# Per-head logits by way of DRAM instead of selector matmuls, in a fused sliding-window attention and gated-MLP kernel

## The chip, the cores and the metric

The kernel runs on one core of a Trainium2 chip. The metric is device time in microseconds (us), the median of several executions. A core has TensorE (PE in the profile, the matmul array), VectorE (DVE), ScalarE (ACT), GpSimd (POOL) and SyncE (SP, which here issues nearly all DMA; ACT has two entries in the profile's list of issues). The profile lists each engine's instructions apart, and for a wait it names the instruction or the DMA that ended it. The program is written as a list of steps. A scheduler in the build lays the steps of each engine into one static order.

The kernel before took 1630.06 to 1631.79 us in its four runs beside the changed kernel.

## The reference, cut to what matters

```python
def _A_ref(x, wqkv, wo):                  # attention: H = 32 heads of 32 columns
    W, dil = 8, 2                         # each token looks at 8 positions, 2 apart
    ...                                   # q, k, v from x @ wqkv; kg, vg: k, v at the 8 positions
    logits = einsum("bhsd,bhswd->bhsw", q, kg) * scale
    attn = softmax(where(mask, logits, -1e9), axis=-1)
    return einsum("bhsw,bhswd->bhsd", attn, vg) ... @ wo

def _B_ref(x, W_gate, W_up, W_down):      # D = 1024, F = 3584
    gate = x @ W_gate;  up = x @ W_up
    return (relu(gate) * up) @ W_down

x = x + _A_ref(_layernorm(x), wqkv, wo)   # S = 2048 tokens
x = x + _B_ref(_layernorm(x), ...)
x = x + _A_ref(...);  x = x + _B_ref(...) # the same two again
```

## The kernel before

The 2048 tokens are cut into four blocks of 512, and the pair of layers runs twice, so there are eight blocks, 0 to 7. TensorE works through them without a pause: q/k and v projections, output projection (wo), gate/up, down. The attention of block n+1 is computed on DVE while TensorE does the gate/up stage of block n. A gate/up stage has 28 steps. Each step is two groups of eight 128x512 matmuls (acc_g, acc_u), a ReLU on ACT and one product on DVE, called hT. The product is what frees the PSUM buffer of acc_u.

Below are the parts that the change and the argument touch; cuts are marked with "...".

```python
psum = tile_pool(name="psum", bufs=6, space=PSUM)     # acc_g, acc_u, acc_q, acc_k, ... share six buffers

def red_mm(n, prod, first, last):         # selector matmuls: sum the 32 columns of each head
    ...                                   # L: logits, partition = (token quarter, head)
    for wh in range(2):
        for tq in range(TPB):
            mm(st["L"][32*tq:32*tq+32, WH*wh:WH*(wh+1), :], lhsT=sel[:],   # sel is 128x32
               rhs=prod[:, WH*wh:WH*(wh+1), tq*P:(tq+1)*P], ..., tile_position=(0, 32*tq))

def softmax(n):
    Lt = st["L"]                                                            # in PSUM
    ...
    nc.vector.tensor_reduce(m[:], Lt[:].rearrange("p w t -> p t w"), axis=AX.X, op=ALU.max)
    nc.vector.tensor_tensor(d[:], Lt[:], _ap(m, 0, [[0, W], [1, P]]), op=ALU.subtract)
    nc.scalar.activation(d[:], d[:], ACT.Exp, scale=scale)
    ...                                                                     # ssum, reciprocal rs, a
def pv_steps(n): ...       # 8 steps: attention times v, and its sum over the window, all on DVE

def gu_steps(n, ln):
    def f_(j):
            ...
            for nm in ("g", "u"):
                acc = psum.tile([P, BLK], F32, tag="acc", name=f"acc_{nm}")
                ...                                                         # eight matmuls
                if nm == "g":
                    r = pool["hid"].tile([P, BLK], BF16, tag="r", name="r", bufs=3)
                    tail_act[0] = nc.scalar.activation(r[:], acc[:], ACT.Relu).ins
            nc.vector.tensor_tensor(hold["hT"][:, j, :], accs["u"][:], r[:], op=ALU.mult)

def sp_dma(dst, src, transpose=False):    # all on SyncE, in the order of the program's text:
    with tc.issue_after(tail_sp[0]):      # issue_after fixes the order of two instructions
        tail_sp[0] = start(dst, src).ins  # of one engine, and nothing else

# where the steps are emitted (n: the block whose gate/up starts at "at"; us)
        spread(gu, at, 2 * GRP)           # GRP = 1.73, one group of eight matmuls
        ...
        elif n + 1 < NN:
            ev.append((at + 0.1, reds_n[n + 1]))
            ev.append((at + 0.2, lambda n=n: softmax(n + 1)))
            spread(pv_steps(n + 1), at + 12.0, 6.5)
            ev.append((at + 72.0, store_o(n + 1)))
            ev.append((at + 72.1, load_o(n + 1)))
```

## Time and profile before

| | before |
|---|---|
| time, median | 1630.3 us |
| span of the profiled run | 1628.4 us |
| TensorE busy | 1618.6 us |
| all waits of TensorE on other engines | 3.3 us |
| DVE busy | 1062.6 us |

The first lines of the profile page of the kernel before (part 1, busy time; part 2, two of the strips of 40 slices, in tenths; part 4, the chain that ended last):

```profile
PE 1618.6 (99%) x7589; PEld 782.2 (48%) x7638; DVE 1062.6 (65%) x926; ACT 506.1 (31%) x1050; POOL 255.7 (16%) x220
...
DVE  5799899985497927949179492894818958211211
...
PEclk9999999999999999999999999999999999999999
...
PE 95%; DVE 4%; issue 1%; DMA 0%; POOL 0%; DVEq 0%
```

TensorE is the bound. DVE is free a third of the time on average, but the strip shows that it works in bursts, at 90% or more in some slices. Here is the full list of TensorE's waits (line, tile, what released it; total us, times, longest):

```profile
PE scratch L129 <- DVE ones L296: 1.5, 1, 1.5
PE dacc L129 <- DVE x L700: 0.8, 1, 0.8
PE acc_v L129 <- DVE xnT_first L103: 0.6, 1, 0.6
PE tp L364 <- DVE xn_first L103: 0.4, 1, 0.4
```

Three of the four lie in the first 10 us. Nothing on DVE delays the gate/up stages. The reason is in DVE's timeline at the start of such a stage (start, duration, operation, in brackets the idle time before it and what ended it). The softmax comes right after the first product, and every product stands close behind the matmuls that feed it (the fourth, at 346.36, is the latest of those shown, by 2.8 us):

```profile
332.57 0.69 DVE L673 TENSOR_TENSOR hT<-acc_u,r 128x512 bf16<-128x512 f32 x1 [2.83 <-PE acc_u L129]
333.18 1.21 DVE L565 TENSOR_REDUCE m<-L 128x128 f32<-128x1024 f32 x1
...
336.68 0.69 DVE L673 TENSOR_TENSOR hT<-acc_u,r 128x512 bf16<-128x512 f32 x1 [1.02 <-PE acc_u L129]
337.28 1.90 DVE L570 TENSOR_REDUCE ssum<-d 128x128 f32<-128x1024 f32 x1
...
341.35 0.68 DVE L673 TENSOR_TENSOR hT<-acc_u,r 128x512 bf16<-128x512 f32 x1
341.95 4.48 DVE L603 TENSOR_TENSOR pv<-a,vhm 128x4096 bf16<-128x4096 bf16 x2
346.36 0.68 DVE L673 TENSOR_TENSOR hT<-acc_u,r 128x512 bf16<-128x512 f32 x1
```

What a selector group costs is read from TensorE's timeline. The distance from acc_u to the next acc_g is 1323.85 - 1321.48 = 2.37 us with a selector group between them, where a group of eight alone takes 1.73, so the selector group costs about 0.65:

```profile
1321.48 1.89 PE L129 MATMUL acc_u<-xnT_b,w_u 128*128 128x512 bf16 x8
1323.30 0.62 PE L129 MATMUL L<-s,sel 128*32 128x512 bf16 x8
1323.85 1.90 PE L129 MATMUL acc_g<-xnT_b,w_g 128*128 128x512 bf16 x8
```

### The profile page before, as it was taken

Reading aid. Unit: us, or ns where it says so; the run is one execution under the profiler, and the core shown is the slowest. Engines: PE = TensorE matmul, PEld = TensorE weight load, DVE = VectorE, ACT = ScalarE, POOL = GpSimd, SP = SyncE. Lnnn points to the kernel's source line nnn. Section 1 sums busy time; section 2 is a strip of 40 time slices with the busy share of each in tenths; the row PEclk is TensorE's granted clock in tenths of the full one; section 3 lists DMA queues with packets and bytes.
Section 4 is the critical chain, followed back from the end, with each engine's and each line's share of the span. In section 5 each row is a group of like instructions: output and inputs, shape, how many; then the busy total and the mean of one; then the engine's idle time right before and its main releaser. Section 6 shows DMA issues by size and latency. Waiting matters only on the chain.

```text
span 1628.4 us, 18703 instructions
## 1 busy us (share of the span) xinstructions
PE 1618.6 (99%) x7589; PEld 782.2 (48%) x7638; DVE 1062.6 (65%) x926; ACT 506.1 (31%) x1050; POOL 255.7 (16%) x220
## 2 busy tenths in 40 slices
PE   9999999999999999999999999999999999999999
PEld 6644445444544445444454444544445444444444
DVE  5799899985497927949179492894818958211211
ACT  4754313243241513405134051331513311131110
POOL 2421003310250102201052010520105100000000
PEclk9999999999999999999999999999999999999999
DMA  9579656746476485664857647577484764655451
GB/s 303 93 203 252 167 177 199 192 156 200 136 215 175 155 233 171 184 175 150 229 181 185 187 150 225 162 203 212 151 231 154 194 205 155 206 164 172 156 168 65
DMA packets 371463, 296.83 MB, mean 182 GB/s; under 512 B 142512, under 2 KB 351664, under 8 KB 370480
## 3 DMA queue, kind: packets, MB, share of 16 engines
q1 hardware_dynamic: 371088, 295.23, 63.2%
q8 instruction: 60, 0.98, 0.3%
q10 hardware_dynamic: 288, 0.39, 0.1%
q14 instruction: 27, 0.22, 0.0%
HBM read 256.77 MB, written 21.00 MB: 171 GB/s over the span
## 4 chain that ended last, share of the span: by engine, by line
PE 95%; DVE 4%; issue 1%; DMA 0%; POOL 0%; DVEq 0%
PE acc_g L129 24%; PE acc_u L129 24%; PE dacc L129 22%; PE acc_v L129 7%; PE acc_k L129 6%; PE acc_q L129 6%; PE acc_wo L129 6%; DVE t L541 2%; DVE ac L551 1%; PE L L129 1%; DVE pv L603 0%; DVE x L648 0%; DVE pv L604 0%; DVE ac L541 0%; DMA x<-in_A_x_dram 0%
## 5 line engine op out<-in xcount | busy, mean ns | idle before, releaser
L129 PE MATMUL acc_g<-xnT_b,w_g 128*128 128x512 bf16 x1792 | 423.4, 379 | 0.0
L129 PE MATMUL acc_u<-xnT_b,w_u 128*128 128x512 bf16 x1792 | 423.3, 379 | 0.0
L129 PE MATMUL dacc<-w_d,hT 128*128 128x512 bf16 x1759 | 386.5, 379 | 2.5 <-DVE x L700 0.8
L672 ACT ACTIVATE r<-acc_g 128x512 bf16<-128x512 f32 x224 | 133.4, 596 | 747.1 <-PE acc_g L129 746.0
L673 DVE TENSOR_TENSOR hT<-acc_u,r 128x512 bf16<-128x512 f32 x224 | 153.7, 687 | 315.1 <-PE acc_u L129 313.5
L129 PEld LDWEIGHTS <-hT 128*128 128x128 bf16 x1792 | 175.4, 98 | 212.3 <-issue 1.0
L129 PEld LDWEIGHTS <-w_g 128*128 128x128 bf16 x1792 | 174.8, 98 | 212.7 <-issue 3.0
L129 PEld LDWEIGHTS <-w_u 128*128 128x128 bf16 x1792 | 175.4, 98 | 211.4
L541 DVE TENSOR_TENSOR t<-q,k 128x2048 f32<-128x2048 bf16 x84 | 191.7, 2290 | 8.6 <-ACT k L480 5.8
L551 DVE TENSOR_TENSOR ac<-ac,t 128x2048 f32<-128x2048 f32 x84 | 191.7, 2282 | 0.4
L485 POOL COPY kh<-k 128x14 bf16<-128x14 bf16 x64 | 81.2, 1273 | 471.9 <-ACT k L480 471.8
L700 DVE TENSOR_TENSOR x<-dacc,x 128x512 bf16<-128x512 f32 x64 | 42.5, 687 | 164.0 <-PE dacc L129 164.0
L603 DVE TENSOR_TENSOR pv<-a,vhm 128x4096 bf16<-128x4096 bf16 x64 | 145.2, 2282 | 0.0
L129 PE MATMUL acc_wo<-w_o,oT 128*128 128x512 bf16 x496 | 111.0, 379 | 0.8
L245 POOL TENSOR_TENSOR st_b<-st_b,neg_half 128x1 f32<-128x1 f32 x29 | 56.4, 1956 | 288.6 <-ACT st_b L244 288.6
L245 POOL TENSOR_TENSOR st_a<-st_a,neg_half 128x1 f32<-128x1 f32 x32 | 41.9, 1315 | 319.2 <-ACT st_a L244 319.1
L484 POOL COPY k<-kh 128x14 bf16<-128x14 bf16 x48 | 70.5, 1469 | 65.9 <-DVE t L541 43.8
L129 PEld LDWEIGHTS <-oT 128*128 128x128 bf16 x512 | 50.0, 98 | 60.4
L604 DVE TENSOR_TENSOR pv<-pv 128x2048 bf16<-128x2048 bf16 x64 | 77.4, 1215 | 0.2
L476 ACT CAST q<-acc_q 128x512 bf16<-128x512 f32 x64 | 37.3, 583 | 73.2 <-PE acc_q L129 73.2
L240 ACT ACTIVATE xn_b<-x 128x1024 bf16<-128x1024 bf16 x29 | 30.3, 1045 | 89.3 <-DVE x L648 89.3
L480 ACT CAST k<-acc_k 128x512 bf16<-128x512 f32 x64 | 37.3, 583 | 63.0 <-PE acc_k L129 62.8
(131 smaller groups left out, 1209.1 us busy)
## 6 DMA issues: line engine op xcount, KB each, us to landing
w_g<-in_B_W_gate_dram SPq DMA_DIRECT2D x56, 1024.0 KB, 7.0
w_u<-in_B_W_up_dram SPq DMA_DIRECT2D x56, 1024.0 KB, 5.4
w_d<-in_B_W_down_dram SPq DMA_DIRECT2D x48, 1024.0 KB, 5.8
w_o<-in_A_wo_dram SPq DMA_DIRECT2D x16, 1024.0 KB, 7.2
vhm<-v_d SPq DMA_DIRECT2D x32, 284.0 KB, 6.9
v_d<-vT SPq DMA_DIRECT2D x8, 1024.0 KB, 10.0
oT<-o_d SPq DMA_DIRECT2D x32, 256.0 KB, 4.4
w_d<-in_B_W_down_dram SPq DMA_DIRECT2D x16, 512.0 KB, 4.0
```

The source lines that it names most:

```text
L129: tail_pe[0] = nc.tensor.matmul(*args, **kwargs).ins
L245: nc.gpsimd.tensor_tensor(rstd, vpe, neg_half[:, 0:1], op=ALU.pow)
L476: tail_act[0] = nc.scalar.copy(q[:], acc[:]).ins
L484: nc.gpsimd.tensor_copy(k[:, 0:HALO], khalo[n - 1][:, c, :])
L485: nc.gpsimd.tensor_copy(khalo[n][:, c, :], k[:, BLK:BLK + HALO])
L541: nc.vector.tensor_tensor(t[:], i0, i1, op=ALU.mult)
L551: nc.vector.tensor_tensor(o, ac[:], t[:], op=ALU.add)
L603: nc.vector.tensor_tensor(tt[:], a_bc, v_sh, op=ALU.mult)
L604: nc.vector.tensor_tensor(tt[:, 0:4], tt[:, 0:4], tt[:, 4:8], op=ALU.add)
L672: tail_act[0] = nc.scalar.activation(r[:], acc[:], ACT.Relu).ins
L673: nc.vector.tensor_tensor(hold["hT"][:, j, :], accs["u"][:], r[:], op=ALU.mult)
L700: nc.vector.tensor_tensor(xs, ac[t], xs, op=ALU.add)
```

## The change

The intent is to take small costs off TensorE, the bound. Blocks 1 to 7 no longer use selector matmuls. Their products s go to DRAM (1 MB) and come back head-major (four loads of 256 KB in runs of 256 bytes), and DVE, which has already added the 32 columns of a head down to four partial sums, adds these four with two additions (the "head sum", u). Block 0 keeps the selector matmuls, but in two groups of four chunks. The first transposes write two PSUM tiles instead of one. The down stage's second half takes two accumulators from the logits' PSUM banks, which are free then. The last accumulator is split in two, and the last stage stores its pieces by itself. Block 1's o goes to DRAM in three stores instead of one. Below is the diff, cut:

```diff
-    ev.append((t_gu0 + 58.1, red1))
-    ev.append((t_gu0 + 58.2, lambda: softmax(1)))
+    ev.append((t_gu0 + 51.0, store_s(1)))
+    ev.append((t_gu0 + 56.0, load_s(1)))
+    ev.append((t_gu0 + 61.0, lambda: softmax(1)))
...
         elif n + 1 < NN:
-            ev.append((at + 0.1, reds_n[n + 1]))
-            ev.append((at + 0.2, lambda n=n: softmax(n + 1)))
-            spread(pv_steps(n + 1), at + 12.0, 6.5)
-            ev.append((at + 72.0, store_o(n + 1)))
-            ev.append((at + 72.1, load_o(n + 1)))
+            ev.append((at - 2.0, store_s(n + 1)))
+            ev.append((at + 3.0, load_s(n + 1)))
+            ev.append((at + 9.0, lambda n=n: softmax(n + 1)))
+            spread(pv_steps(n + 1), at + 21.0, 6.5)
+            ev.append((at + 80.0, store_o(n + 1)))
+            ev.append((at + 80.1, load_o(n + 1)))
...
+    def store_s(n):
+        def f():
+            sp_dma(s_d[n % 2][:], att[n]["s"][:].rearrange("p w t -> p (w t)"))
+    def load_s(n):
+        def f():
+            ...
+            for tq in range(TPB):
+                src = bass.AP(tensor=sd.tensor, offset=sd.offset + tq * P,
+                              ap=[[DG * W * BLK, H], [BLK, DG * W], [1, P]])
+                sp_dma(s4[32 * tq:32 * tq + 32, :, :, :].rearrange("p d w t -> p (d w) t"), src)
+    def head_sum(n):
+        s4 = att[n].pop("s4")
+        u = work.tile([P, DG // 2, W, P], F32, tag="ac", name=f"u_{n}", bufs=1)
+        nc.vector.tensor_tensor(u[:], s4[:, 0:2], s4[:, 2:4], op=ALU.add)
+        nc.vector.tensor_tensor(u[:, 0], u[:, 0], u[:, 1], op=ALU.add)
+        return u[:, 0]
     def softmax(n):
-        Lt = st["L"]
+        Lt = st["L"] if n == 0 else head_sum(n)
...
-        return [mult(c) for c in range(KC)], [red(c) for c in range(KC)]
+        return [mult(c) for c in range(KC)], [red(0, KC // 2), red(KC // 2, KC)]
...
+                    if half == 1:
+                        pair = psum_l.tile([P, TPB // 2, BLK], F32, tag="L", name="dacc_pair")
...
+            if n == NN - 1 and half == 1:
+                cols[-1:] = [(TPB - 1, 0, SLAB // 2), (TPB - 1, SLAB // 2, SLAB)]
```

More of the change, by code (lines that the diff above doesn't have):

```diff
@@ L156 @@
     o_d = dram.tile([NT, H, DH, P], BF16, name="o_d")
+    s_d = [dram.tile([P, W * BLK], BF16, name=f"s_d{i}") for i in range(2)]
     zpad = const.tile([P, KC, HALO], BF16, name="zpad")
@@ L360, in turn, with copy @@
         def turn(t):
-            tps[t] = psum.tile([P, KC, P], BF16, tag="acc", name="tp")
+            tps[t] = [psum.tile([P, KC // 2, P], BF16, tag="acc", name=f"tp{h}") for h in range(2)]
             for c in range(KC):
                 with pe_group():
-                    tail_pe[0] = nc.tensor.transpose(tps[t][:, c, :], xna[:, t, c * P:(c + 1) * P], ident[:]).ins
-        def copy(t, eng, c0=0, c1=KC):
+                    tail_pe[0] = nc.tensor.transpose(tps[t][c // (KC // 2)][:, c % (KC // 2), :],
+                                                     xna[:, t, c * P:(c + 1) * P], ident[:]).ins
+        def copy(t, eng, h):
             f = nc.vector.tensor_copy if eng == "v" else nc.scalar.copy
-            on(eng, f, hold["xnT"][:, t, c0:c1, :], tps[t][:, c0:c1, :])
+            on(eng, f, hold["xnT"][:, t, h * (KC // 2):(h + 1) * (KC // 2), :], tps[t][h][:])
         warm = small("warm")
@@ L382, in ln_first @@
         apply(1)
-        copy(0, "v", 0, KC // 2)
-        copy(0, "a", KC // 2, KC)
+        copy(0, "a", 1)
+        copy(0, "a", 0)
         turn(1)
         act_vpe(2, st1)
-        copy(1, "v", 0, KC // 2)
-        copy(1, "a", KC // 2, KC)
+        copy(1, "v", 0)
+        copy(1, "a", 1)
         bn(3, 0)
@@ L393, in ln_first @@
         apply(3)
-        hold["later"] = {2: (lambda: (turn(2), copy(2, "a"))),
-                         4: (lambda: (turn(3), copy(3, "v", 0, KC // 2), copy(3, "a", KC // 2, KC)))}
+        hold["later"] = {2: (lambda: (turn(2), copy(2, "a", 0), copy(2, "v", 1))),
+                         4: (lambda: (turn(3), copy(3, "v", 0), copy(3, "a", 1)))}
         return hold
@@ L510, in f @@
             def f():
-                prods[c] = work.tile([P, W, BLK], BF16, tag="t", name=f"prod_{c}")
+                if c in (3, 4):
+                    prods[c] = work.tile([P, W, BLK], BF16, tag="t", name=f"prod_{c}")
+                else:
+                    prods[c] = big_tile([P, W, BLK], f"prod_{c}")
                 i0, i1 = qk_bcast(n, c, 0, W)
@@ L514, in mult, with red @@
             return f
-        def red(c):
+        def red(c0, c1):
             def f():
-                red_mm(n, prods.pop(c), c == 0, c == KC - 1)
+                for c in range(c0, c1):
+                    red_mm(n, prods.pop(c), c == 0, c == KC - 1)
             return f
-        return [mult(c) for c in range(KC)], [red(c) for c in range(KC)]
+        return [mult(c) for c in range(KC)], [red(0, KC // 2), red(KC // 2, KC)]
     def prod_sum_steps(n):
@@ L551, in add @@
             nc.vector.tensor_tensor(o, ac[:], t[:], op=ALU.add)
-        def red():
-            red_mm(n, st["s"], True, True)
-        return [mult(h, c) for h in range(2) for c in range(KC)], red
+        return [mult(h, c) for h in range(2) for c in range(KC)]
+    def store_s(n):
+        def f():
+            sp_dma(s_d[n % 2][:], att[n]["s"][:].rearrange("p w t -> p (w t)"))
+        return f
+    def load_s(n):
+        def f():
+            sd = s_d[n % 2]
+            s4 = work.tile([P, DG, W, P], BF16, tag="t", name=f"s4_{n}")
+            for tq in range(TPB):
+                src = bass.AP(tensor=sd.tensor, offset=sd.offset + tq * P,
+                              ap=[[DG * W * BLK, H], [BLK, DG * W], [1, P]])
+                sp_dma(s4[32 * tq:32 * tq + 32, :, :, :].rearrange("p d w t -> p (d w) t"), src)
+            att[n]["s4"] = s4
+        return f
+    def head_sum(n):
[4 more added lines that the diff above has]
+        return u[:, 0]
     def softmax(n):
         st = att[n]
-        Lt = st["L"]
+        Lt = st["L"] if n == 0 else head_sum(n)
         if n % NB == 0:
@@ L564, in softmax @@
         m = soft.tile([P, P], F32, tag="m", name="m")
-        nc.vector.tensor_reduce(m[:], Lt[:].rearrange("p w t -> p t w"), axis=AX.X, op=ALU.max)
+        nc.vector.tensor_reduce(m[:], (Lt[:] if n == 0 else Lt).rearrange("p w t -> p t w"), axis=AX.X, op=ALU.max)
         d = soft.tile([P, W, P], F32, tag="d", name="d")
-        nc.vector.tensor_tensor(d[:], Lt[:], _ap(m, 0, [[0, W], [1, P]]), op=ALU.subtract)
+        nc.vector.tensor_tensor(d[:], Lt[:] if n == 0 else Lt, _ap(m, 0, [[0, W], [1, P]]), op=ALU.subtract)
         nc.scalar.activation(d[:], d[:], ACT.Exp, scale=scale)
@@ L682, in f_ @@
         def f_(half, s8):
+            cols = [(t, 0, SLAB) for t in range(TPB)]
+            if n == NN - 1 and half == 1:
+                cols[-1:] = [(TPB - 1, 0, SLAB // 2), (TPB - 1, SLAB // 2, SLAB)]
             def f():
@@ L685, in f @@
                 if s8 == 0:
-                    accs[half] = [psum.tile([P, BLK], F32, tag="acc", name=f"dacc{t}")[:] for t in range(TPB)]
+                    own = {}
+                    if half == 1:
+                        pair = psum_l.tile([P, TPB // 2, BLK], F32, tag="L", name="dacc_pair")
+                        own = {2: pair[:, 0, :], 3: pair[:, 1, :]} if len(cols) == TPB else {2: pair[:, 0, :]}
+                    accs[half] = [own[i] if i in own else psum.tile([P, BLK], F32, tag="acc", name=f"dacc{i}")[:]
+                                  for i in range(len(cols))]
                 ac = accs[half]
@@ L689, in f @@
                 wsl = slab[("d", n, half, s8)]
-                for t in range(TPB):
+                for a, (t, c0, c1) in zip(ac, cols):
                     with pe_group():
@@ L693, in f @@
                             j = 8 * s8 + jl
-                            mm(ac[t], lhsT=hT[:, j, t * P:(t + 1) * P], rhs=wsl[:, jl, :],
+                            mm(a[:, c0:c1], lhsT=hT[:, j, t * P:(t + 1) * P], rhs=wsl[:, jl, c0:c1],
                                start=(j == 0), stop=(j == FC - 1))
                 if s8 == NSL - 1:
-                    for t in range(TPB):
+                    for a, (t, c0, c1) in zip(ac, cols):
                         xt = x_tiles[b * TPB + t]
-                        xs = xt[:, half * SLAB:(half + 1) * SLAB]
-                        nc.vector.tensor_tensor(xs, ac[t], xs, op=ALU.add)
+                        xs = xt[:, half * SLAB + c0:half * SLAB + c1]
+                        nc.vector.tensor_tensor(xs, a[:, c0:c1], xs, op=ALU.add)
+                        if n == NN - 1:
+                            row = (b * TPB + t) * P
+                            col = half * SLAB + c0
+                            sp_dma(out_dram[row:row + P, col:col + c1 - c0], xs)
             return f
@@ L724 @@
     ln_b = {}
-    reds_n = {}
     ln_a[0] = ln_first()
@@ L747, in ln2 @@
             ev.append((turn_at, turn()))
-    GAP0 = 2.05
+    GAP0 = 1.9
     t_v0 = 9.5
@@ L778 @@
         ev.append((t_qk0 + GAP0 * (2 * c + 2.0), mults[c]))
-        if c < KC - 2:
-            ev.append((t_qk0 + GAP0 * (2 * c + 4.5), reds[c]))
+    ev.append((t_qk0 + GAP0 * 9.5, reds[0]))
     spread(load_v_steps(0), t_qk0 + 19.0, 1.0)
-    ev.append((t_qk1 + 0.5 * GRP, reds[KC - 2]))
-    ev.append((t_qk1 + 2.5 * GRP, reds[KC - 1]))
-    ev.append((t_qk1 + 2.6 * GRP, lambda: softmax(0)))
-    ln1(2, t_qk0 + 10.0, t_qk1 + 5.0, True, 4.5)
+    ev.append((t_qk1 + 1.5 * GRP, reds[1]))
+    ev.append((t_qk1 + 1.6 * GRP, lambda: softmax(0)))
+    ln1(2, t_qk0 + 10.0, t_qk1 + 7.5, True, 4.5)
     spread(qk_steps(1, ln_a[1], "qk01"), t_qk1, GRP)
@@ L795 @@
     ev.append((t_wo0 + 3.0, store_v(2)))
-    sums1, red1 = prod_sum_steps(1)
+    sums1 = prod_sum_steps(1)
     spread(sums1[:4], t_qk1 + 50.0, 4.4)
@@ L814 @@
         if n == 0:
-            spread(pv_steps(1), at + 66.0, 5.5)
-            ev.append((at + 105.0, store_o(1)))
-            ev.append((at + 105.1, load_o(1)))
-        elif n + 1 < NN:
-            ev.append((at + 0.1, reds_n[n + 1]))
-            ev.append((at + 0.2, lambda n=n: softmax(n + 1)))
-            spread(pv_steps(n + 1), at + 12.0, 6.5)
-            ev.append((at + 72.0, store_o(n + 1)))
-            ev.append((at + 72.1, load_o(n + 1)))
+            spread(pv_steps(1), at + 66.5, 5.5)
+            ev.append((at + 90.0, store_o(1, 0, 4)))
+            ev.append((at + 101.0, store_o(1, 4, 6)))
+            ev.append((at + 108.0, store_o(1, 6, 8)))
+            ev.append((at + 108.1, load_o(1)))
+        elif n + 1 < NN:
+            ev.append((at - 2.0, store_s(n + 1)))
[4 more added lines that the diff above has]
+            ev.append((at + 80.1, load_o(n + 1)))
         if n + 2 < NN:
@@ L829 @@
             spread(qk_steps(n + 2, ln_a[n + 2], ("qk", n + 2)), at, GRP)
-            sums, reds_n[n + 2] = prod_sum_steps(n + 2)
-            spread(sums, at + GRP * (K_STEP[0] + 1.0), 4.4)
+            spread(prod_sum_steps(n + 2), at + GRP * (K_STEP[0] + 1.0), 4.4)
             at += 2 * GRP * KC
@@ L847 @@
         at += GRP * FC
-        if n >= NN - NB:
+        if NN - NB <= n < NN - 1:
             ev.append((at + 4.0, store_x(n)))
```

## The prediction

> **What bounds the kernel.** TensorE: 1618.6 of 1628.4 us busy (part 1 of the page), 95% of the chain that ended last (part 4). Eight 128x512 matmuls take 1.727 us, gapless (timeline). TensorE's waits on other engines sum to 3.3 us (the list of waits); after the start at most 0.76: block 0's second down half, on a DVE addition that frees an accumulator. DVE is 65% busy, in bursts.
>
> **Saved (estimates from the timeline), all critical.**
> - Selector groups (eight 32-column matmuls that sum logits over a head) cost more than their 0.44 us of array time: in blocks 1 to 7 each costs 0.65; seven go: 4.5 us. In block 0 each costs 0.70; eight become two groups of four, so six mode switches of 0.27 go: 1.6. [...]
> - Accumulators in the free L banks: 0.8. Start, where an ACT copy waits 1.6 us behind a DVE copy: 0.4. End, a last addition of half width (0.69 to about 0.42) and a store of 64 KB, not 256: 0.8.
>
> Sum: about 8 us (0.5%).
>
> **Added.** A 1 MB store (its like, o_d, lands in 10 us), four 256 KB loads in 256-byte runs (like oT, 4.4 us), DVE sums of 2.28 + 1.2 us per block. Little is critical by itself.
>
> **Moved: the cost.** [...] In the built program, block 1's head sum follows the 24th of 28 gate/up products, where the softmax now follows the 17th; in blocks 2 to 7 it follows the 8th, where the softmax now follows the 1st. The scheduler expects logits late; I expect them some 15 to 20 us before DVE asks. Behind each head sum overdue work stands ahead of the next product: in block 1 softmax and four pv groups, 28 us; in the others two pv groups and a third multiplication, 11 us. A product frees acc_u's PSUM buffer; with six buffers TensorE gets at most about 8.6 us past it, then stalls. I walked the static order by its semaphores with durations from the trace: 1629.2 for the kernel before (measured span 1628.4), 1680.9 for the changed one:
> - block 1: TensorE waits 11 us in the q/k stage, 5 us for a q/k weight slab whose issue is held behind the o store, 8 us for oT: 24 us;
> - blocks 2 to 7: 4 to 7 us each, mostly two waits, before about the 15th and 17th gate/up steps: 36 us.
>
> Net: +52 us. If the clock drops after long waits, some us more; faster DMA takes at most 5 away.
>
> **Prediction:** 1682 us, range 1666 to 1696. Faster by over 2%: 0.02; within 2%: 0.08; slower by over 2%: 0.90.
>
> **What would show it.** Right: selector groups only twice, early; TensorE waits on DVE of 3 to 4 and 2 to 3 us in each later gate/up stage, and 20 to 28 us lost between block 0's gate/up and block 1's wo; before each head sum DVE waits for acc_u, not DMA; no dacc waits. Wrong: no PE waits in gate/up.
>
> **What would make it wrong.** Slack in acc_u's buffers that I miscounted, so that DVE catches up (about 1622 then); DMA contention that makes logits land later than DVE asks (slower still).

The forecast's sum: about 8 us saved against 60 us of waits, +52 us. The 0.44 us and the 0.27 us of a "mode switch" (from 128x128 to selector matmuls and back) agree with the timelines of both kernels: one selector group by itself costs 0.70 us (before, 31.60 to 35.75 us, less two groups of 1.727), four in a row 1.99 (after, 40.44 to 45.88, less the same), which makes 0.43 for each group and 0.27 for each switch. The 8.6 us is five groups of 1.727, an estimate. The remark on the clock has no number; after a wait of 4.03 us the granted clock measured 0.51. The half-width addition took 0.415 us.

## The result, and the profile after

| | before | after |
|---|---|---|
| time, median | 1630.3 us | 1687.45 us |
| span | 1628.4 us | 1686.6 us |
| TensorE's waits on other engines | 3.3 us | 50.2 us |
| TensorE busy | 1618.6 us | 1633.0 us |
| bytes moved by DMA | 296.83 MB | 311.49 MB |

The ratio is 1.0349, with a 95% interval of 1.0332 to 1.0367. Ratios in this document are the mean time of one kernel's fast runs over that of the other's fast runs of the same rounds, so they are not quite the ratio of the medians quoted.

The page of the changed kernel, the same parts:

```profile
PE 1633.0 (97%) x7610; PEld 788.8 (47%) x7610; DVE 1092.3 (65%) x941; ACT 502.7 (30%) x1051; POOL 256.9 (15%) x220
...
DVE  5799579949498585945859367693766927621111
...
PEclk9999998999999999999999999999999999999999
...
PE 85%; DVE 11%; issue 2%; DMA 1%; POOL 1%; ACT 0%; SPq 0%; DVEq 0%
```

TensorE's share of the chain fell by ten points and DVE's rose by seven. TensorE is busy 14 us longer, although it has seven selector groups fewer. The clock granted to it was 0.987 on average, against 1.000 before. Its waits (the short ones left out):

```profile
PE acc_g L129 <- DVE hT L699: 22.4, 8, 4.3
PE acc_k L129 <- DVE hT L699: 10.0, 1, 10.0
PE acc_u L129 <- DVE hT L699: 5.2, 4, 2.1
PE acc_k L129 <- DMA w_('qk', 2)_k<-in_A_wqkv_dram: 4.3, 1, 4.3
PE acc_wo L129 <- DMA oT<-o_d: 4.2, 1, 4.2
```

The first and third lines (27.6 us, 12 waits) lie in the gate/up stages of blocks 1 to 6, in which the attention of blocks 2 to 7 is computed; from here on "blocks 2 to 7" and "block 2's stage" mean these stages. Each has 3.4 to 5.6 us of waits, 4.6 on average. The other three, 18.5 us, lie between block 0's gate/up stage and block 1's wo. The wait on dacc is gone, as intended.

DVE's timeline in the stage that held the softmax of block 2:

```profile
379.03 0.69 DVE L699 TENSOR_TENSOR hT<-acc_u,r 128x512 bf16<-128x512 f32 x1 [2.76 <-PE acc_u L129]
379.64 2.28 DVE L580 TENSOR_TENSOR u<-s 128x2048 f32<-128x2048 bf16 x1
381.95 1.22 DVE L581 TENSOR_TENSOR u<-u 128x1024 f32<-128x1024 f32 x1
383.21 1.91 DVE L591 TENSOR_REDUCE m<-u 128x128 f32<-128x1024 f32 x1
...
391.59 0.68 DVE L699 TENSOR_TENSOR hT<-acc_u,r 128x512 bf16<-128x512 f32 x1
392.19 4.48 DVE L629 TENSOR_TENSOR pv<-a,vhm 128x4096 bf16<-128x4096 bf16 x2
396.59 2.35 DVE L630 TENSOR_TENSOR pv<-pv 128x2048 bf16<-128x2048 bf16 x2
...
402.94 0.68 DVE L699 TENSOR_TENSOR hT<-acc_u,r 128x512 bf16<-128x512 f32 x1
```

The first line is the 8th product; DVE had been idle 2.76 us before it, waiting for TensorE. Then come the head sum, the softmax and a pile of pv work. The last line is the 11th product; 10.75 us of pv work, from 392.19 to 402.94, stand between it and the 10th. TensorE delivers a step every 3.455 us (the spacing of the products before the head sum), so the 11th could have started at 379.03 + 3 x 3.455 = 389.4, and it is 13.5 us late. TensorE's timeline shows what that costs:

```profile
397.75 1.89 PE L129 MATMUL acc_u<-xnT_b,w_u 128*128 128x512 bf16 x8
403.67 3.48 PE L129 MATMUL acc_g<-xnT_b,w_g 128*128 128x512 bf16 x8 [4.03 <-DVE hT L699]
406.98 1.89 PE L129 MATMUL acc_u<-xnT_b,w_u 128*128 128x512 bf16 x8
```

TensorE stops for 4.03 us until the 11th product is done, and the eight matmuls after it take 3.48 us instead of 1.89: the clock granted from 403.6 to 407 us was 0.51, and 1.00 before and after. (ACT stands still too, 63.9 us in 18 waits of its ReLU for hT, because r has three buffers and a product frees one. No wait of TensorE ends on that ReLU, but no run gave r more buffers.) The second cost shows in the matmul groups (busy time, mean ns of one matmul), first before, then after:

```profile
L129 PE MATMUL acc_g<-xnT_b,w_g 128*128 128x512 bf16 x1792 | 423.4, 379 | 0.0
L129 PE MATMUL acc_u<-xnT_b,w_u 128*128 128x512 bf16 x1792 | 423.3, 379 | 0.0
```

```profile
L129 PE MATMUL acc_g<-xnT_b,w_g 128*128 128x512 bf16 x1792 | 430.2, 384 | 22.4 <-DVE hT L699 22.4
L129 PE MATMUL acc_u<-xnT_b,w_u 128*128 128x512 bf16 x1792 | 427.3, 382 | 5.2 <-DVE hT L699 5.2
```

These two groups took 10.8 us longer. Block 2's q and k groups, whose stage follows block 0's gate/up, took 3.5 us longer (33.1 against 29.6), and the wo group 1.7 us (113.5 against 111.8 in a run with as many records, the first below). That is 16 us of slow matmuls. The sum: 46.9 us more waits and 16 us of slow matmuls, less about 7.4 us of savings (measured below; the wait on dacc, counted twice here, and a seventh selector group, not counted, about cancel), is 55.5 of the 58.2 us by which the span grew. The last 3 us are not assigned.

The logits were in time. In this stage the four loads were issued between 357.97 and 362.3 us, and no load of this kind took more than 9.6 us to land, so they were there by 372 at the latest; DVE asked for them at 379.64.

### The profile page after: what moved, and what is told of

Read it like the earlier page. It is cut to its first block, busy times and chain, and to the rows that moved or that the text cites. A ratio compares the mean times of both kernels' runs of the same rounds, so it can differ in the third digit from the quotient of the medians.

```text
span 1686.6 us, 18775 instructions
## 1 busy us (share of the span) xinstructions
PE 1633.0 (97%) x7610; PEld 788.8 (47%) x7610; DVE 1092.3 (65%) x941; ACT 502.7 (30%) x1051; POOL 256.9 (15%) x220
## 2 busy tenths in 40 slices
DMA packets 402598, 311.49 MB, mean 185 GB/s; under 512 B 171856, under 2 KB 382160, under 8 KB 400848
## 4 chain that ended last, share of the span: by engine, by line
PE 85%; DVE 11%; issue 2%; DMA 1%; POOL 1%; ACT 0%; SPq 0%; DVEq 0%
PE acc_u L129 19%; PE acc_g L129 18%; PE dacc L129 18%; PE acc_wo L129 7%; PE acc_v L129 7%; PE acc_k L129 6%; PE acc_q L129 6%; PE dacc_pair L129 5%; DVE pv L629 3%; DVE pv L630 2%; POOL kh L487 1%; DVE u L580 1%; DVE ssum L596 1%; DVE m L591 1%; DVE pv L631 1%
## 5 line engine op out<-in xcount | busy, mean ns | idle before, releaser
L129 PE MATMUL acc_g<-xnT_b,w_g 128*128 128x512 bf16 x1792 | 430.2, 384 | 22.4 <-DVE hT L699 22.4
L129 PE MATMUL dacc<-w_d,hT 128*128 128x512 bf16 (+1 forms) x1400 | 301.6, 375 | 0.0
L487 POOL COPY kh<-k 128x14 bf16<-128x14 bf16 x64 | 93.0, 1458 | 435.8 <-ACT k L482 435.7
L735 DVE TENSOR_TENSOR x<-dacc,x 128x512 bf16<-128x512 f32 (+1 forms) x50 | 32.2, 675 | 159.9 <-PE dacc L129 159.9
L129 PE MATMUL acc_wo<-w_o,oT 128*128 128x512 bf16 x512 | 113.5, 383 | 4.2 <-DMA oT<-o_d 4.2
L129 PE MATMUL dacc_pair<-w_d,hT 128*128 128x512 bf16 x420 | 95.9, 379 | 0.0
L246 POOL TENSOR_TENSOR st_b<-st_b,neg_half 128x1 f32<-128x1 f32 x29 | 47.6, 1651 | 291.1 <-ACT st_b L245 291.1
```

The costliest lines, as they stand in the source:

```text
L129: tail_pe[0] = nc.tensor.matmul(*args, **kwargs).ins
L246: nc.gpsimd.tensor_tensor(rstd, vpe, neg_half[:, 0:1], op=ALU.pow)
L487: nc.gpsimd.tensor_copy(khalo[n][:, c, :], k[:, BLK:BLK + HALO])
L735: nc.vector.tensor_tensor(xs, a[:, c0:c1], xs, op=ALU.add)
```

## The experiments

Three theories are told apart:

- **A, order.** The scheduler places the head sum late in DVE's static order and puts overdue pv work ahead of the products. TensorE runs out of PSUM buffers and waits. The clock drops after long waits (to 0.51 after the 4.03 us above).
- **B, traffic.** The trip through DRAM slows TensorE's weights or delivers the logits late.
- **C, added work.** The head sum (3.5 us on DVE for each block) and the slower maximum (1.91 us from SBUF, 1.21 from PSUM) cost the time by themselves.

| run | what it is | median us | ratio to before (95%) |
|---|---|---|---|
| e1_nodram | after, without the trip | 1627.3 | 0.9981 (0.9968 to 0.9993) |
| e2_pinned | after, DVE order of blocks 2 to 7 fixed | 1645.9 | 1.0095 (1.0082 to 1.0109) |
| e3_traffic | before, with the trip's traffic | 1687.75 | 1.0353 (1.0338 to 1.0367) |
| e4_traffic_pin | the same, DVE order held | 1630.1 | 0.9998 (0.9982 to 1.0013) |
| e5_act_queue | after, trip issued by ScalarE | 1640.8 | 1.0057 (1.0042 to 1.0073) |
| e6_best | trip for blocks 2 to 7 only, order fixed | 1623.0 | 0.9954 (0.9942 to 0.9967) |
| e7_five_slots | after, five PSUM buffers | 1703.3 | 1.0445 (1.0431 to 1.046) |
| e8_late_order | before, softmax emitted late | 1650.3 | 1.0123 (1.0109 to 1.0136) |
| e9_late_no_pile | after, pv emitted later | 1657.3 | 1.0163 (1.0149 to 1.0177) |
| e10_block1_old | after, block 1 as before | 1663.7 | 1.0204 (1.0188 to 1.022) |
| e11_simple_best | e10 with e5's edit | 1623.9 | 0.9962 (0.9949 to 0.9974) |

All eleven gave correct results.

### e1: the change without the trip

```diff
-        Lt = st["L"] if n == 0 else head_sum(n)
+        Lt = st["L"]                                # selector matmuls in every block
-            ev.append((at - 2.0, store_s(n + 1)))
-            ev.append((at + 3.0, load_s(n + 1)))
-            ev.append((at + 9.0, lambda n=n: softmax(n + 1)))
-            spread(pv_steps(n + 1), at + 21.0, 6.5)
+            ev.append((at + 0.1, lambda n=n: reds_n[n + 1]()))
+            ev.append((at + 0.2, lambda n=n: softmax(n + 1)))
+            spread(pv_steps(n + 1), at + 12.0, 6.5)
 ...                                                 # block 1's softmax and the o stores of blocks 2 to 7 likewise
```

> The changed kernel without the trip through DRAM: blocks 1 to 7 sum their logits on TensorE and run softmax where the kernel before does; the rest of the change stays (block 0 grouping, paired transposes, accumulators, tail). Theory A (the static order of DVE behind the late head sum costs the time): all of the loss goes and the small savings show, 1625 to 1628 us, TensorE waits under 4 us in all. Theory C (the small parts themselves cost something): over 1632 us. B (contention by the trip's DMA) expects the same as A here.

It took 1627.3 us against 1630.4 for the kernel before in the same rounds, and the four waits left sum to 2.5 us. So the rest of the change saves 3.1 us, and the whole loss belongs to the trip and what it brings with it.

### e2: the same trip and the same work, in another order

```diff
-        nc.vector.tensor_tensor(u[:], s4[:, 0:2], s4[:, 2:4], op=ALU.add)
+        dv(nc.vector.tensor_tensor, u[:], s4[:, 0:2], s4[:, 2:4], op=ALU.add)
...                                                   # dv: issue_after the previous dv; likewise softmax, pv, hT
-            ev.append((at + 9.0, lambda n=n: softmax(n + 1)))
-            spread(pv_steps(n + 1), at + 21.0, 6.5)
+            ev.append((at + 17.2, lambda n=n: softmax(n + 1)))      # up to d
+            ev.append((at + 20.7, lambda n=n: softmax2(n + 1)))     # from ssum on
+            spread(pv_steps(n + 1), at + 24.0, 6.5)
```

> The changed kernel with the same DMA trip and the same DVE work; only the order of DVE in blocks 2 to 7 is fixed by order edges, so that head sum, softmax and pv stand between the gate/up products one part at a time. Block 1 stays as it is in the changed kernel. Theory A: the waits of acc_g on the hT product in blocks 2 to 7 go, block 1's 24 us stay: 1645 to 1652 us. Theory B (contention, or late logits): 1680 to 1690, unchanged. Theory C (the added DVE work itself): unchanged too, since all of it is still there.

It took 1645.9 us: 41.5 us of the loss are gone. No wait on hT is left in blocks 2 to 7, their matmul groups are back at 423.3 us, and block 1's waits of 10.0 and 4.8 us are still there. The only wait on hT in its list is that of block 1:

```profile
PE acc_k L133 <- DVE hT L102: 10.0, 1, 10.0
```

DVE was busy 1102.5 us, no less than in the changed kernel. Traffic, latency and added work are all present, so none of them is enough by itself in blocks 2 to 7.

### e3 and e4: the traffic alone, with a free and with a held order

```diff
+            ev.append((at - 2.0, store_s(n + 1)))    # the same 1 MB, from tiles that exist anyway
+            ev.append((at + 3.0, load_s(n + 1)))     # four copies DRAM to DRAM, runs of 256 bytes
             ev.append((at + 0.1, reds_n[n + 1]))     # all else as in the kernel before
```

e4 has the same edit, and holds the DVE instructions of blocks 2 to 7 in a fixed order with the chain of e2. Its expectation calls this the order of the kernel before. The trace shows that this is so for the softmax only: each pv step stands whole between two products, where the kernel before has its instructions one by one among them.

> The kernel before, with the trip's traffic added in blocks 2 to 7 (1 MB stored and four copies of 256 KB in runs of 256 bytes at the same places), read by nobody; no DVE work is added. The scheduler, left free, moves DVE's static order because of it. Walk of its order: 1678. Theory A: 1670 to 1690 us, with TensorE waits on hT. Theory B: also slower. Theory C: 1630. To be read beside the next run.

> The same added traffic as in the run before, but the DVE instructions of blocks 2 to 7 are held by order edges in the order of the kernel before. Theory A: 1629 to 1633 us, TensorE waits under 6 us in all, although the DMA traffic is the same. Theory B (traffic by itself slows TensorE or delays its slabs): as slow as the run before, 1670 or more.

With the free order the traffic alone costs as much as the whole change: 1687.75 us. With the order held it costs nothing: 1630.1 us. The DMA instructions of the two kernels stand in the same order on SyncE. Their TensorE waits, e3 first (without the small ones of the start), then e4 in full:

```profile
PE acc_g L129 <- DVE hT L690: 25.5, 4, 6.4
PE acc_u L129 <- DVE hT L690: 19.1, 2, 9.6
```

```profile
PE scratch L133 <- DVE ones L302: 1.5, 1, 1.5
PE tp L370 <- DVE xn_first L107: 1.3, 2, 1.0
PE acc_v L133 <- DMA w_v<-in_A_wqkv_dram: 1.2, 1, 1.2
PE dacc L133 <- DVE x L727: 0.8, 1, 0.8
```

So theory B falls: with the order held, the bytes do no harm. (Nobody reads these copies, so e4 says nothing of late logits; that half of B falls by the trace above and by e2 and e6, which read the real ones.) This also says how a DMA that nobody waits for can cost 57 us. In e3 nothing on DVE depends on the copies. Still, the built order of the stage with block 2's softmax has sixteen pv instructions between the 8th and the 9th product, where the kernel before has three. The break stands where a new weight slab is needed. A gate or up slab serves four steps, SyncE issues its DMAs in the order of the text, and the trip stands just before and after the gate slab of steps 9 to 12. It fits this that the scheduler prices the copies high, expects the slabs behind them late, and fills the gap that it sees with pv work. That reason is argued from the positions; how the scheduler prices a DMA was not measured.

### e5: the trip on another queue

```diff
-            sp_dma(s_d[n % 2][:], att[n]["s"][:].rearrange("p w t -> p (w t)"))
+            nc.scalar.dma_start(s_d[n % 2][:], att[n]["s"][:].rearrange("p w t -> p (w t)"))
-                sp_dma(s4[32 * tq:32 * tq + 32, :, :, :].rearrange("p d w t -> p (d w) t"), src)
+                nc.scalar.dma_start(s4[32 * tq:32 * tq + 32, :, :, :].rearrange("p d w t -> p (d w) t"), src)
```

> The changed kernel with one edit: the store of the logits and the four loads are issued by ScalarE, not by SyncE, whose queue also issues the weight slabs in a fixed order. Same bytes, same DVE work. The scheduler then puts the head sum of blocks 2 to 7 after the 3rd and 4th product instead of the 8th, with at most three pv steps between products. Theory A (order): the walk of the new order gives 1641; expected 1640 to 1652 us, nearly all that is left being block 1 (about 18 us, q/k and oT). Theory B (the trip's latency and traffic): unchanged, 1680 to 1690, or slower, as the logits would be asked for earlier. Theory C (the added work): unchanged.

It took 1640.8 us. The waits of acc_u on hT are 4.9 us in six pieces, the longest 1.4; the rest is block 1 (oT 4.5, acc_q 3.0, a weight slab 1.5). Two edited lines, which change neither bytes nor DVE work, take 46.7 of the 57 us back. In the built order the two additions of the head sum now follow the 3rd and 4th products in the stages of blocks 2 and 3 and the 1st and 2nd in the later ones, not the 8th; block 1's head sum follows the 19th, not the 24th. This supports the reading that the place in SyncE's fixed order of DMAs is what pushed it back. (The changed kernel's SyncE does stand still before the loads, from its issue at 351.32 to 357.97 us in block 2's stage, and the up slab behind them is issued at 363.41; but no wait of TensorE on a gate or up slab is in the list.)

### e7: five buffers instead of six

```diff
-    psum = ctx.enter_context(tc.tile_pool(name="psum", bufs=6, space=bass.MemoryType.PSUM))
+    psum = ctx.enter_context(tc.tile_pool(name="psum", bufs=5, space=bass.MemoryType.PSUM))
```

> The changed kernel with five PSUM buffers for accumulators instead of six; the static order of DVE in the gate/up stages stays nearly the same. If TensorE stalls because it runs out of acc_u buffers behind the pile on DVE, each long wait grows by up to one product step of TensorE (a gate and an up group, about 3.5 us), at least by 1.7: the waits of acc_g, acc_u and of q/k on hT, 37.6 us together with six buffers, become 50 to 65 us, and the whole 1700 to 1715 us (walk: 1696.7 against 1680.9). The accumulators of the down stage cost some 6 us of this, as they would in the kernel before. If the waits come from late DMA, the hT waits stay near 38.

It took 1703.3 us. The waits on hT became 28.1 (acc_u), 16.8 (acc_q) and 10.0 (acc_g), 54.9 us together, where six buffers gave 37.6; the wait in block 1 grew from 10.0 to 16.8 (the wait of 4.3 for the weight slab behind it is gone), and the dacc waits came to 5.3. The waits depend on the number of buffers, as they must if TensorE stops because none is free. (DVE's order was not held here; it differs from the changed kernel's in 28 of 941 places, with every head sum behind the same product.)

### e8: a late order without the trip

```diff
-            ev.append((at + 0.1, reds_n[n + 1]))                     # in the kernel before
-            ev.append((at + 0.2, lambda n=n: softmax(n + 1)))
-            spread(pv_steps(n + 1), at + 12.0, 6.5)
+            ev.append((at + 2 * GRP * 7 + 0.1, reds_n[n + 1]))
+            ev.append((at + 2 * GRP * 7 + 0.2, lambda n=n: softmax(n + 1)))
+            spread(pvs[:3], at + 2 * GRP * 9 + 0.1, 0.01)
+            spread(pvs[3:], at + 21.0 + 3 * 6.5, 6.5)
 ...                                                                  # block 1: after the 24th product
```

> The kernel before, without any trip and any added traffic or DVE work; only the moments of emission change: selector group and softmax of block 1 after the 24th product with the pv steps piled behind it, of blocks 2 to 7 after the 8th with three pv steps piled ahead of a product. Theory A: it loses time with nothing else of the change present: walk 1654, expected 1648 to 1665 us. B and C: 1630.

The time, 1650.3 us, lies in the expected range, but for another reason than I had for blocks 2 to 7. The loss is nearly all one wait of 18.7 us for oT in block 1 (the granted clock was 0.993 over the run); in blocks 2 to 7 no wait is left at all:

```profile
PE acc_wo L129 <- DMA oT<-o_d: 18.7, 1, 18.7
```

That is instructive, because the built order of block 2 from the 8th to the 11th product is the changed kernel's, instruction for instruction, without the two additions of the head sum. DVE's timeline there:

```profile
377.59 0.69 DVE L673 TENSOR_TENSOR hT<-acc_u,r 128x512 bf16<-128x512 f32 x1 [2.76 <-PE acc_u L129]
378.20 1.22 DVE L565 TENSOR_REDUCE m<-L 128x128 f32<-128x1024 f32 x1
...
386.37 0.68 DVE L673 TENSOR_TENSOR hT<-acc_u,r 128x512 bf16<-128x512 f32 x1
386.97 4.48 DVE L603 TENSOR_TENSOR pv<-a,vhm 128x4096 bf16<-128x4096 bf16 x2
...
397.72 0.68 DVE L673 TENSOR_TENSOR hT<-acc_u,r 128x512 bf16<-128x512 f32 x1
```

The pile is the same (10.75 us from 386.97 to 397.72). TensorE has a selector group behind the 8th step here, which costs it 0.64 us, so the 11th product could have started at 377.59 + 10.365 + 0.64 = 388.6; it is 9.1 us late, with no wait of TensorE. In the changed kernel it was 13.5 us late and TensorE waited 4.03. Of the difference of 4.4 us, 3.8 is on DVE (the head sum, 3.5 us, and the slower maximum, 0.7, less some idle time), and 0.6 is the selector group that TensorE no longer has. So TensorE has some 9.5 us of slack here (13.5 - 4.03), the pile alone nearly uses it up, and almost all that comes on top of the pile is paid.

### e9: the late head sum without the pile

```diff
-            spread(pv_steps(n + 1), at + 21.0, 6.5)
-            ev.append((at + 80.0, store_o(n + 1)))
+            spread(pv_steps(n + 1), at + 40.0, 5.5)
+            ev.append((at + 86.0, store_o(n + 1)))
```

> The changed kernel; only the pv steps of blocks 2 to 7 are emitted later and closer (from 40 us, 5.5 us apart, instead of from 21, 6.5 apart), so that in the built order the head sum still follows the 8th product with all its added work, but the overdue pile ahead of the 11th product is gone. Block 1 unchanged. If the pile on top of the head sum is what costs: walk 1652.5, expected 1648 to 1656 us, long TensorE waits in blocks 2 to 7 gone (each under 1.5 us). If the late head sum is enough by itself: TensorE waits stay at 3 to 4 us per block, 1675 or more.

It took 1657.3 us, 1 us above the expected range. The head sum still follows the 8th product, with all its work. The longest wait on hT in blocks 2 to 7 is 1.3 us; they sum to 5.4 us:

```profile
PE acc_u L129 <- DVE hT L699: 5.4, 6, 1.3
```

Some DMA waits are new: w_o 1.6 and three q/k slabs of 1.4, 1.1 and 0.7 us (that they come from the later o is argued, not tested). With e8 this answers the question for blocks 2 to 5: the pile without the head sum makes TensorE wait not at all, the late head sum without the pile causes no wait on hT, and both together 4.3 to 4.8 us in each stage. In the stages of blocks 6 and 7 the late head sum alone leaves 2.7 us each, of 5.6 and 3.4 in the changed kernel. The late head sum is still not free: e9 took 11.4 us more than e2.

### e10: block 1 put back

```diff
-    ev.append((t_gu0 + 51.0, store_s(1)))
-    ev.append((t_gu0 + 56.0, load_s(1)))
-    ev.append((t_gu0 + 61.0, lambda: softmax(1)))
+    ev.append((t_gu0 + 58.1, lambda: red_mm(1, att[1]["s"], True, True)))
+    ev.append((t_gu0 + 58.2, lambda: softmax(1)))
 ...                                                 # pv, store_o and load_o of block 1 as before
```

> The changed kernel with block 1 alone put back: its logits are summed on TensorE and its softmax and o store stand where the kernel before has them; blocks 2 to 7 as in the changed kernel. It separates the loss of block 1 from that of the others. From the trace of the changed kernel, block 1 should hold about 20 us of waits and 6 us of slow matmuls: expected 1660 to 1666 us, with the waits of acc_g and acc_u on hT in blocks 2 to 7 staying near 27 us in all. If block 1 was not separable, over 1672.

It took 1663.7 us, so block 1 holds 1687.45 - 1663.7 = 23.7 us. The waits of acc_g (21.6) and acc_u (5.1) on hT remain, as expected. The two parts are separate: 23.7 here and 41.5 in e2 sum to 65.2, and the changed kernel stands 64.4 us above the version below that has neither.

### e6 and e11: versions that keep the gain

e6 puts block 1 back as in e10 and fixes the order of blocks 2 to 7 as in e2. e11 is e10 with the two lines of e5, and no order edges.

> A version meant to beat both: block 1 sums its logits on TensorE as before; blocks 2 to 7 take the trip through DRAM, with the order of DVE fixed as in the pinned run. Theory A: the savings come through without the stalls, 1621 to 1625 us, about 5 under the run without the trip at most (six selector groups at 0.65 us: 3.9). Theory C (head sum and slower max are paid on the way): not below the run without the trip, 1627 or more.

> The run before, with the trip of blocks 2 to 7 issued by ScalarE: no order edges on DVE at all. Walk 1624.6; expected 1624 to 1629 us, some short TensorE waits on hT (under 1.5 us each, about 3 in all) being what remains against the version with fixed order (1623.0).

e6 took 1623.0 us, ratio 0.9954 (0.9942 to 0.9967), and e11 1623.9 us, ratio 0.9962 (0.9949 to 0.9974). Both beat both kernels; the gain over the kernel before is under half a per cent. The waits of e6, in full:

```profile
PE scratch L133 <- DVE ones L301: 1.5, 1, 1.5
PE tp L369 <- DVE xn_first L107: 1.3, 1, 1.3
PE acc_v L133 <- DMA w_v<-in_A_wqkv_dram: 0.9, 1, 0.9
PE tp L369 <- DVE mean L107: 0.4, 1, 0.4
```

e11's expected short waits on hT did not appear. e6 lies 4.3 us under e1 by the medians, in another set of rounds; six selector groups at 0.65 are 3.9. So theory C falls as a cause by itself: with the right order the head sum is hidden whole.

## Why the prediction was right

The prediction said 1682 us (range 1666 to 1696), slower by over 2%. The result is 1687.45. Its main step, that the static order of DVE and not the DMA decides, was shown by e2, e3 against e4, and e5. Point by point:

- **What bounds the kernel.** Right; TensorE was at 99%.
- **Savings of about 8 us.** 3.1 us (e1) for block 0, accumulators, start and end, predicted as 1.6 + 0.8 + 0.4 + 0.8 = 3.6; and about 4.3 us for six selector groups, predicted as 3.9. Seven of them were predicted as 4.5. In detail: TensorE's timelines give block 0 as 1.6 (from the start of the first q group to that of the last, 24.69 to 78.64 us before, 24.90 to 77.23 after), the dacc wait of 0.8 is gone, and the end from the last matmul on fell from 3.9 to 3.4 us. The start saved nothing visible: v began at 10.06 us after a wait of 0.92 on its weights, not at 9.69.
- **Logits in time.** Right in kind: in block 2's stage they were there at least 7.7 us before DVE asked (372 against 379.64), where I expected 15 to 20.
- **Block 1, 24 us of waits.** The three waits came in the named places, on hT (10.0, predicted 11), the weight slab (4.3, predicted 5) and oT (4.2, predicted 8), and acc_q added 1.3 on ACT. The block cost 23.7 (e10). By the trace this is less lucky than it looks: oT landed at 287.2 us, behind DVE's last addition for o (done at 281.0), its store and its loads, and the slow q/k matmuls (3.5 us) ran while TensorE would else have waited for it. They took the place of waiting; only the slow wo matmuls behind (1.7) came on top. No run tested this.
- **Blocks 2 to 7, 36 us of waits.** Measured 27.6; with the slow matmuls they cost 41.5 us (e2). Two waits of 3 to 4 and 2 to 3 us were predicted, before the 15th and 17th steps. In blocks 2 to 5 the first came, with 4.0 to 4.3 us; the second was 0.8 us at most. The slow matmuls between the two (1.6 us in block 2) make TensorE later by themselves, which shortens the second; a slack of some 9.5 us instead of 8.6 should shorten the waits too. How much each does was not tested. In blocks 6 and 7 most of the waiting came earlier, in the 12th and 14th steps.
- **"If the clock drops after long waits, some us more."** The term that was left without a number: the slow matmuls measured 16 us. The waits were 13 us smaller than predicted (46.9 more, where 60 were predicted), and the whole still 5 us larger (65.2 by e2 and e10, against 60). As some slow matmuls only took the place of waits, the 16 us are not what the clock added; what it added by itself was not measured. That the two errors nearly cancelled in the total is in part luck.
- **"Little is critical by itself"**, said of the added DMA and sums. Right for the DMA (e4). For the sums it holds in a good order (e6, e11), but in the order as built they are what goes over the slack (e8): the prediction put the stall down to 11 us of pv pile, and the pile alone costs nothing in blocks 2 to 7; it takes both.
- **"The scheduler expects logits late."** Not the whole reason: e3 has no logits from DRAM and its order is just as bad. The queue of weight slabs behind the trip is the likelier reason (e5), but what the scheduler computes was not seen.

Two things that the prediction rests on can be read from the traces. A selector group costs more than the 0.43 us that each of four in a row adds: 0.65 us between gate/up groups and 0.70 by itself in block 0, and the grouping in block 0 saved 1.6 us; what the excess of 0.27 us for each switch is made of, no run shows. And DVE did not take a product ahead of its turn: the 11th product had its inputs at 389.3 us (its ReLU was done at 388.5, its acc_u at 389.3) and started at 402.94, behind 10.75 us of pv work that it did not need.

## What to carry to other kernels

Where a scheduler orders an engine that is not the bound, a moved wait or a new DMA can reorder it in stages far away: compare the static order of every engine before and after, and ask how much work may stand between two instructions that free a buffer of the bound engine. Add up all that stands there, old and new, against that slack; here nothing was paid until it was exceeded, and then nearly everything was, with a slow clock (0.50 to 0.55 after most of the long waits) in part on top. If the order is the trouble, fix it by order edges, or issue the new DMA from another engine's queue, before giving up the change.

## What the traces show of the clock, the maximum and a late product

- After long waits the granted clock was low. In the changed kernel it was 0.50 to 0.53 in the 3.4 us after five waits on hT (4.03, 4.33, 4.02, 3.81 and 2.08 us), and the next eight matmuls took 3.42 to 3.57 us, not 1.89. After a sixth, of 4.04 us, it was 0.75 at first, and two groups of eight took 2.42 and 3.09 us. In block 1 it was 0.50 after the waits of 9.96 and 4.28 us, and 0.55 after that of 4.15 us. After every wait of 3.8 us or more in e2, e9 and e10 the next matmuls were slow too (eight in 3.48 to 3.57 us, or four in 1.86 to 1.93, where four take 1.03), and after none of 1.55 us or less in after, e2, e9 and e10 (the start of the program left aside). Between these it was mixed: a wait of 2.08 us was followed by slow matmuls in e10 as well (eight in 3.38 us), but waits of 2.46 us (e2) and 2.91 us (e9) were not (the next 32 took 7.08 us, 0.22 each). So the length of the wait alone does not decide; what else does, no run here shows.
- The same maximum, of 128x1024 fp32 read across its rows, took 1.21 us from PSUM and 1.91 us from SBUF. Why PSUM was faster, no run here shows.
- What a late product costs, with six PSUM buffers shared by gate and up: TensorE ran on while a product was 9.1 us late (e8), and stopped 4.03 us when it was 13.5 us late.
